# Q transposed contiguously and read by TensorE in the order of time, with chain steps ranked ahead of relus

## The chip, the cores and the metric

The kernel runs on one core of a Trainium2 chip. The core has five engines with a queue each: TensorE (PE in the profile, its weight loads PEld), VectorE (DVE), ScalarE (ACT), GpSimd (POOL) and SyncE (SP). Each engine takes its instructions in the order in which the program wrote them and waits where an operand isn't there yet; DMAs are issued from the queues of SP, ACT and POOL. The metric is the device time of one execution in microseconds, as the median of several runs.

## The reference

A gated recurrence (gateloop) over 768 steps for 4 batches and 8 heads of 48, with a complex decay clipped to magnitude 0.999, and behind it a dense block with relu squared over all 3072 tokens:

```python
mag = np.sqrt(a_re * a_re + a_im * a_im)
scale = np.minimum(mag, 0.999) / (mag + 1e-06)
a_re_n, a_im_n = (a_re * scale, a_im * scale)
for t in range(S):                       # S = 768
    new_re = ar * S_re - ai * S_im       # ar, ai: a_re_n, a_im_n at t
    new_im = ar * S_im + ai * S_re
    S_re, S_im = (new_re + k_t v_t^T, new_im)
    y[:, :, t] = q_t @ S_re
x = y.transpose(0, 2, 1, 3).reshape(3072, 384)
h = x @ w_in                             # 384 x 2048
g = np.maximum(h, 0.0) ** 2
out = g @ w_out                          # 2048 x 384
```

## The kernel before

All work is in `fast_path`; at its end a flag is computed from sums that were collected on the way, and a general version would run only if that flag were set.

The 3072 tokens are cut into six units of L = 512 tokens (n = 0 to 5), and a unit into W = 4 blocks of C = 128. For each unit there are three kinds of work.

`chain(n)` (rank CHAIN = 2) loads the decays, normalises them (`roots`, `normalise`), forms running products inside groups of four steps (`inner`), turns the totals with TensorE (`totals`, through the helper `turned`, L993, with copies by ScalarE at L1008), scans them on VectorE (`scan`), and turns them back (`back`, L993 and L1102). Its last part, `apply`, multiplies the running products into q and k (L1151 to L1189, with ScalarE's L1159, L1164 and L1169 between), and `gather` sends k to KC by DMA.

`pairs(n)` (rank PAIR = 1) works on two heads at a time, four pairs per unit. In units 0 and 1 (n < EARLY = 2) `turn_pe` transposes Q and K with TensorE (L1285) and ScalarE copies them to QT (L1288). From unit 2 on `turn` does it with VectorE's 32x32 stream transpose (L1262, two per pair: j = 0 is Q, j = 1 is K), and DMAs from SP and ACT put the blocks into QT (L1267). A row of four consecutive time steps lies side by side in the source, so each transpose writes its 32 results with a step of four elements, so that QT is in order of time: index (t c), c being the step within four. Then `score` multiplies K's columns with Q's (L1305), VectorE applies the causal mask (L1308), `keep` forms the block states (TensorE L1334, copies and sums by ScalarE L1344 and VectorE L1348), and `mix` adds scores times v (L1359) and state times Q (L1363) in PSUM. ScalarE copies the result to yt (L1371) and DMAs carry it to xT (L1378). Score and mix read Q as TensorE's moving operand and K as its weights.

`dense(n, grp)` (rank DENSE = 3) is the dense block of the unit in two groups of 256 tokens: x @ w_in (L1400), relu and square on ScalarE (L1431, L1432, rank (0, n), the first rank of all), and the second product, plain in unit 0 (L1446), by blocks in the others (L1497, with sums on VectorE at L1512 and L1521). It uses three PSUM banks d0 to d2. In unit 0 the weights, which come as 64-bit words, are also converted in pieces: ScalarE L809 and L813, VectorE L815 and L822.

What sets the order is a planner, the class `Plan`. Each piece of work is a `step` with an engine, an estimated duration, the keys it reads and writes, and a rank. The planner plays the steps through with these durations, fixed delays between engines (HOP, MARGIN, SLACK), a rate for DMAs, and takes on each engine the step of lowest rank among those that are ready; on VectorE and ScalarE it may hold an engine of low-ranked work a little (HOLD) for a step ranked ahead of URGENT = (2, 0.2). The program is then written out in that order, so every engine's queue is fixed before the run. The choice is made here:

```python
n = min((n for n in wait[e] if at[n] <= t), key=lambda n: (steps[n][4], n))
```

`steps[n][4]` is the rank. So a duration in a `step` call changes no instruction, only where instructions stand in the queues.

Of the kernel before, what the change touches and what calls it, by code (L numbers as in the profile page):

```python
# [598 lines left out]
def fast_path(ctx, tc, q, k, v, a_re, a_im, moe_w_in, moe_w_out, out, flag):  # L599
# [127 lines left out]
        return n / 1200.0 + 0.10  # L727

    SUM = 0.22
    SCORE = 0.7  # L730
    checked = []

    def step(*args, **kw):
        return plan.add(*args, **kw)

    def check(*args, **kw):
        checked.append(step(*args, **kw))
# [60 lines left out]
    def convert(i):  # L798
        held = [("a", 1)] if SOON <= i < NPIECE else []
        _, t, keys, dst, n, wk = piece(i)  # L800
        t3 = t.rearrange("p m (f two) -> p m f two", two=2)
        lo, hi = t3[:, :, :, 0], t3[:, :, :, 1]
        bits = dst.bitcast(U32)
        rank = (W2, 0.6) if i >= NPIECE else (W1, 0.3)
        def part(dtype, i):
            return t.bitcast(dtype).rearrange("p m (f four) -> p m f four", four=4)[:, :, :, i]

        step("ACT", ac(PW) + 0.06, keys, [("lo", i), ("lo", i, 0)],
             lambda: act.activation(out=lo, in_=lo, func=AF.Copy, scale=2.0 ** -29), rank)  # L809
        mixed = SOON <= i < 2 * NPIECE - 2  # L810
        if mixed:

            step("ACT", 1.92, keys + [("lo", i)], [("lo", i, 1)], lambda: act.activation(  # L813
                out=part(F16, 1), in_=part(I16, 3), func=AF.Copy, scale=2.0 ** -60), rank)
        step("DVE", ts2(PW), keys + held, wk, lambda: dve.tensor_scalar(  # L815
            out=bits, in0=hi, scalar1=0x07FFFFFF, scalar2=3,
            op0=ALU.bitwise_and, op1=ALU.logical_shift_left), rank)
        if not mixed:
            step("DVE", tt(PW), keys, wk, lambda: dve.scalar_tensor_tensor(
                out=bits, in0=hi, scalar=0xC0000000, in1=bits,  # L820
                op0=ALU.bitwise_and, op1=ALU.bitwise_or), rank)
        step("DVE", tt(PW), keys + [("lo", i, int(mixed))], wk, lambda: dve.tensor_tensor(  # L822
            out=bits, in0=bits, in1=lo, op=ALU.add), rank)
# [72 lines left out]
    def chain(n):  # L896
# [90 lines left out]
        def turned(src, put, by, keys, rk):  # L987
            b = trs[slot["tr"] % 2]
            slot["tr"] += 1

            def go():
                for m in range(NM):
                    pe.transpose(put(bank[b][:, 0:DM], m), src(m), by)  # L993
            step("PE", 0.12 * NM, keys, [(b,)], go, rk)
            return bank[b][:, 0:DM], (b,)

        def natural(t, m):
# [118 lines left out]
        def level():  # L1116
            dve.reciprocal(out=lv[:, n, 0:1], in_=tot[:, n:n + 1])
            dve.tensor_scalar(out=lv[:, n, 1:2], in0=lv[:, n, 0:1], scalar1=-UP * UP,
                              scalar2=None, op0=ALU.mult)
        check("DVE", 0.16, [("tot",)], [("lv", n)], level, ahead)  # L1120

        def squares(j):
            for r in range(2):
# [116 lines left out]
    def pairs(n, which):  # L1240
# [9 lines left out]
        def turn(i):  # L1250
            z = i // 2
            s = take("QT", 3 if 0 < n < ROOM else 2)
            t = QT[s].rearrange("p (i x) -> p i x", i=W)
            got["T", i] = s
            T6 = aq[z].rearrange("p (y j x) -> p y j x", y=2, j=NJ)
            for j in range(2):
                nat = ff[z][:, j * Z:(j + 1) * Z].rearrange(
                    "p (c h j r) -> p c h j r", c=W, h=HH, j=NJ)[:, :, ts(i % 2, 2)]
                dst = T6[:, i % 2].rearrange("p j (k h t c) -> p k c h j t", k=2, h=2, c=W)
                step("DVE", tt(768), [("f", z, 2 * j), ("f", z, 2 * j + 1)],  # L1260
                     [("a", z) if i % 2 == 0 else ("qk", z)],
                     lambda nat=nat, dst=dst, j=j: dve.transpose(out=dst[:, j], in_=nat), rank)  # L1262
            for b in range(W):
                for j in range(NJ):
                    queue = act if j == 2 else sp
                    dma(queue, [("a", z) if i % 2 == 0 else ("qk", z)], [("QT", s, 0), ("QT", s, 1)],
                        lambda b=b, j=j, z=z, t=t, T6=T6, queue=queue: queue.dma_start(  # L1267
                            out=t[32 * j:32 * j + 32, b],
                            in_=T6[32 * b:32 * b + 32, i % 2, j]), rank, 65536,
                        group=(n, i))  # L1270

        def turn_pe(i):
# [5 lines left out]
            for h in range(2):  # L1278
                for j in (1, 0):
# [3 lines left out]
                    def go(h=h, j=j, ps=ps):  # L1283
# [5 lines left out]
                        out=dst, in_=bank[b][0:R].rearrange("p (i t) -> p i t", i=W)), rank,  # L1289
                        group=(n, i))  # L1290

        def score(i, h):
            s = got["T", i]
            T = QT[s].rearrange("p (i k h t) -> p i k h t", i=W, k=2, h=2)[0:R]
            b = "sc%d" % take("sc", 2)
            sa = bank[b].rearrange("p (j t) -> p j t", j=W)
            a = take("A", 3 if 0 < n < ROOM else 2)
            got["A", i, h] = a

            def go():  # L1300
                for j0 in range(0, W, 2):
                    for half in range(2):
                        for j in (j0, j0 + 1):
                            p0, t0 = CH * (half ^ (j % 2)), CH * half
                            pe.matmul(sa[p0:p0 + CH, j, t0:C], lhsT=T[:, j, 1, h, t0:t0 + CH],  # L1305
                                      rhs=T[:, j, 0, h, t0:C], start=True, stop=True)
            step("PE", SCORE, [("QT", s, h)], [(b,)], go, rank, slack=True)
            step("DVE", tt(L) + 0.05, [(b,)], [("A", a)], lambda: dve.tensor_tensor(  # L1308
                out=As[a].rearrange("p (j o t) -> p j o t", o=2, t=C),
                in0=bank[b].rearrange("p (j o t) -> p j o t", o=2, t=C), in1=mask4,  # L1310
                op=ALU.mult), rank)

        def keep(i):
# [10 lines left out]
            for js in ([j for j in need if j < 3], [j for j in need if j == 3]):  # L1324
                if not js:
                    continue
                b = trs[take("tr", 2)]
                ps = bank[b][0:R, 0:8 * D].rearrange("p (j h d) -> p j h d", j=W, h=2)
                last = js == [3]

                def go(js=js, ps=ps):
                    for j in js:
                        for h in range(2):
                            pe.matmul(ps[:, j, h], lhsT=kc[:, j, (2 * i + h) % HH],  # L1334
                                      rhs=v5[:, j, 2 * i + h], start=True, stop=True)
                step("PE", 0.34 * len(js), [("KC%d" % last, z, i % 2), ("v", vs(n))], [(b,)], go,
                     rank, slack=True)

                for j in js:
                    o = new if j == 3 else at[j + 1]  # L1340
                    reads = [(b,)] + ([("S", n % 2, i)] if j == 0 else [("st", s, j)])
                    writes = [("S", (n + 1) % 2, i)] if j == 3 else [("st", s, j + 1)]
                    if at[j] is None:
                        step("ACT", ac(2 * D), reads, writes, lambda o=o, j=j, ps=ps: act.copy(  # L1344
                            out=o, in_=ps[:, j]), rank)
                    else:
                        step("DVE", tt(2 * D) + 0.04, reads, writes,
                             lambda o=o, j=j, ps=ps: dve.tensor_tensor(  # L1348
                                 out=o, in0=ps[:, j], in1=at[j], op=ALU.add), rank)

        def mix(i):
            T = QT[got["T", i]].rearrange("p (i k h t) -> p i k h t", i=W, k=2, h=2)[0:R]
            at, s = got["S", i]
            aa = [As[got["A", i, h]].rearrange("p (j t) -> p j t", j=W) for h in range(2)]

            def go():
                for j in range(W):
                    for h in range(2):
                        pe.matmul(ypair[64 * h:64 * h + D, ts(j, C)], lhsT=v5[:, j, 2 * i + h],  # L1359
                                  rhs=aa[h][:, j], start=True, stop=at[j] is None)  # L1360
                    for h in range(2):
                        if at[j] is not None:
                            pe.matmul(ypair[64 * h:64 * h + D, ts(j, C)], lhsT=at[j][:, h],  # L1363
                                      rhs=T[:, j, 0, h], start=False, stop=True)
            step("PE", 2.0, [("A", got["A", i, h]) for h in range(2)]
                 + [("v", vs(n)), ("QT", got["T", i], 0), ("QT", got["T", i], 1),
                    ("S", n % 2, i)]
                 + [("st", s, j) for j in (1, 2, 3)],
# [23 lines left out]
    def dense(n, grp):  # L1392
# [26 lines left out]
        for f2, b, ps, o, s in blocks:  # L1419
# [10 lines left out]
            def relu(o=o, ps=bank[b]):  # L1430
                act.activation(out=o, in_=ps, func=AF.Relu)  # L1431
                act.activation(out=o, in_=o, func=AF.Square)  # L1432
            step("ACT", 2 * ac(2 * G), [(b, "x"), (b,), (b, "y")],
                 [(b,)] + [("g", s, r) for r in range(4)], relu, (0, n))
        if n >= FAST:
            (seven if joint else eight)(n, grp)
# [56 lines left out]
    def half(n, b, r, h, w, wkeys, first=True, last=True):  # L1493

        def go():
            for j in range(4 * h, 4 * h + 4):
                pe.matmul(bank[b][:, 0:DH], lhsT=g4[:, r, j], rhs=w(j),  # L1497
                          start=first and j == 0, stop=last and j == NT - 1)
        step("PE", 1.32, gk(r, h) + wkeys, [(b,)], go, (DENSE, n))

    def w_lo(c):
        return lambda j: w2[:, j, ts(c, DH)]
# [186 lines left out]
```

## Time and profile before

| | |
|---|---|
| median of 3 runs | 706.53 us (705.7 to 707.09) |
| the profiled execution | 706.77 us, span 705.0 us |
| TensorE busy | 630.2 us (89%) |
| VectorE busy | 557.3 us (79%) |
| ScalarE busy | 339.5 us (48%) |
| mean granted TensorE clock | 0.991 |
| VectorE's stream transposes (L1262) | 32, 47.5 us |
| scores on TensorE (L1305, both shapes and targets) | 768 records |

Times in the profile count from the start of the span. Busy time of an engine leaves out waits. A row of a group names line, engine, operation, output and input with their shapes, then count, total busy time, mean in ns, and the idle time of the engine just before with what ended it. A row of the timeline begins with start and length in us and ends, in brackets, with the idle time before it and what released it. "x32" is a number of records; an fp32 matmul leaves two. A timeline's length of several matmuls goes from the first start to the last end, which is modelled, so matmuls overlap in it.

The first matmuls of any size start some 56 us into the span; units 0 and 1 reach their pairs near 56 and 170 us, units 2 to 5 near 270, 370, 470 and 575 us. After the last pairs, from about 616 us, only the dense block of unit 5 and the collected tests remain.

### The profile page before, as it was taken

How to read it: one execution, taken by the hardware profiler on the slowest of the kernel's cores; microseconds unless marked ns; L12 is line 12 of the kernel's file. 1: busy time of each engine (PE TensorE's matmuls, PEld its weight loads, DVE VectorE, ACT ScalarE, POOL GpSimd, SP SyncE). 2: the span in 40 equal slices, each digit the busy share in tenths (PEclk: the TensorE clock that was granted, in tenths of full speed). 3: DMA queues.
4: the chain of work that ended last, by engine and by line, in shares of the span. 5: the costliest groups of instructions: out<-in, count | busy, mean ns of one | idle time of the engine just before them, and what ended most of it. 6: DMA issues, size and time to landing. Idle time of an engine off the chain costs nothing.

```text
span 705.0 us, 11855 instructions
## 1 busy us (share of the span) xinstructions
PE 630.2 (89%) x4442; PEld 559.2 (79%) x4442; DVE 557.3 (79%) x1125; ACT 339.5 (48%) x586; POOL 96.3 (14%) x166
## 2 busy tenths in 40 slices
PE   0108898999999999989999999999999999999996
PEld 0007775686778999978998898988899988999996
DVE  7999992989787897885999698988887998336721
ACT  6678736865675153336453438435247352032230
POOL 6301140201100010120021030011030011032200
PEclk9999999999999999999999999999999999999999
DMA  9924386111630006562027580045561035287600
GB/s 285 332 99 101 68 224 191 24 45 45 169 98 5 12 16 156 145 168 68 13 66 185 138 178 8 1 101 146 135 164 18 23 92 141 51 279 253 240 3 27
DMA packets 52068, 79.53 MB, mean 113 GB/s; under 512 B 7745, under 2 KB 35073, under 8 KB 52001
## 3 DMA queue, kind: packets, MB, share of 16 engines
q0 software_dynamic: 11712, 40.90, 19.2%
q1 hardware_dynamic: 36160, 32.79, 18.8%
q10 hardware_dynamic: 4128, 4.98, 2.8%
q8 instruction: 37, 0.61, 0.4%
q14 instruction: 31, 0.25, 0.1%
HBM read 48.76 MB, written 4.72 MB: 76 GB/s over the span
## 4 chain that ended last, share of the span: by engine, by line
PE 61%; DVE 26%; DMA 6%; ACT 3%; issue 2%; SPq 1%; ACTq 0%; DVEq 0%
PE d L1400 21%; PE d L1497 20%; PE d L1446 5%; DVE aq L1262 4%; PE sc L1305 4%; DVE f L1189 3%; DMA aq<-in_q_dram 3%; DVE f L1151 3%; PE yp L1359 3%; PE tr L1334 2%; PE yp L1363 2%; DVE g L1512 2%; DVE aq L1155 2%; DVE KC L1038 1%; DMA QT<-aq 1%
## 5 line engine op out<-in xcount | busy, mean ns | idle before, releaser
L1400 PE MATMUL d<-xT,w 128*128 128x256 f32 x1056 | 237.7, 382 | 2.9 <-DMA xT<-yt 2.9
L1400 PEld LDWEIGHTS d<-xT,w 128*128 128x128 f32 x1056 | 199.6, 191 | 30.6 <-DMA xT<-yt 3.3
L1497 PE MATMUL d<-w,g 128*128 128x192 f32 x832 | 144.2, 329 | 0.0
L1497 PEld LDWEIGHTS d<-w,g 128*128 128x128 f32 x832 | 136.0, 191 | 2.1 <-issue 1.3
L1431 ACT ACTIVATE g<-d 128x512 f32<-128x512 f32 x88 | 52.4, 596 | 129.0 <-PE d L1400 111.2
L1432 ACT ACTIVATE g<-g 128x512 f32<-128x512 f32 x96 | 60.6, 631 | 3.0
L1512 DVE TENSOR_TENSOR g<-g 128x512 f32<-128x512 f32 x56 | 37.7, 687 | 30.6 <-ACT g L1432 18.6
L1497 PE MATMUL d<-T,g 128*128 128x192 f32 x336 | 59.6, 330 | 0.0
L1497 PEld LDWEIGHTS d<-T,g 128*128 128x128 f32 x336 | 56.0, 193 | 0.3
L1226 POOL DMA_DIRECT2D KC<-f x52 | 27.6, 545 | 174.9 <-DVE f L1189 125.3
L1458 POOL DMA_DIRECT2D out_dram<-ot x22 | 12.3, 559 | 278.1 <-DVE ot L1521 247.4
L1446 PE MATMUL d<-w,g 128*128 128x384 f32 x128 | 45.5, 505 | 3.1 <-DVE w L822 3.1
L1262 DVE STREAM_TRANSPOSE aq<-f 128x768 f32<-128x768 f32 x32 | 47.5, 1573 | 0.3
L1151 DVE TENSOR_TENSOR f<-aq,xn 128x384 f32<-128x384 f32 (+1 forms) x64 | 45.5, 749 | 1.4 <-ACT xn L1102 1.4
L1371 ACT COPY yt<-yp 112x512 f32<-112x512 f32 x24 | 13.9, 581 | 63.1 <-PE yp L1363 55.7
L1308 DVE TENSOR_TENSOR A<-sc,mask 128x512 f32<-128x512 f32 x45 | 29.8, 685 | 12.5 <-PE sc L1305 12.2
L1446 PEld LDWEIGHTS d<-w,g 128*128 128x128 f32 x128 | 24.4, 197 | 18.7 <-DVE w L822 3.7
L1305 PEld LDWEIGHTS sc<-QT 96*64 96x64 f32 x736 | 34.1, 137 | 5.6 <-issue 3.3
L1305 PE MATMUL sc<-QT 96*64 96x128 f32 (+1 forms) x736 | 37.4, 250 | 0.6 <-DMA QT<-aq 0.3
L964 DVE TENSOR_TENSOR f<-aq 128x384 f32<-128x384 f32 x72 | 36.9, 552 | 0.8
L1521 DVE TENSOR_TENSOR ot<-ot,d 128x192 f32<-128x192 f32 x61 | 20.7, 348 | 20.0 <-PE d L1497 19.7
L1359 PE MATMUL yp<-A,v 128*48 128x128 f32 x320 | 32.4, 277 | 3.5 <-DVE A L1308 3.3
(179 smaller groups left out, 919.5 us busy)
## 6 DMA issues: line engine op xcount, KB each, us to landing
QT<-aq SPq DMA_DIRECT2D x128, 64.0 KB, 2.0
f<-in_moe_w_in_dram POOLq DMA_DIRECT2D x8, 768.0 KB, 6.8
f<-in_moe_w_out_dram POOLq DMA_DIRECT2D x8, 768.0 KB, 6.8
out_dram<-ot POOLq DMA_DIRECT2D x22, 192.0 KB, 2.4
QT<-aq ACTq DMA_DIRECT2D x64, 64.0 KB, 2.1
KC<-f POOLq DMA_DIRECT2D x36, 96.0 KB, 3.4
xT<-yt SPq DMA_DIRECT2D x36, 96.0 KB, 2.6
aq<-in_a_re_dram SPq DMA_DIRECT2D x8, 384.0 KB, 4.1
```

Of the source, the lines that this page charges most:

```text
L964: lambda c=c, j=j: dve.tensor_tensor(out=f[j], in0=a[:, :, :, c - 1], in1=a[:, j, :, c].unsqueeze(1).to_broadcast([C, 2, HH, D]), op=ALU.m ...
L1151: lambda j=j, r=r: dve.tensor_tensor(out=f4[:, j, r], in0=a[:, r], in1=over(j), op=ALU.mult), late[z])
L1262: lambda nat=nat, dst=dst, j=j: dve.transpose(out=dst[:, j], in_=nat), rank)
L1305: pe.matmul(sa[p0:p0 + CH, j, t0:C], lhsT=T[:, j, 1, h, t0:t0 + CH], rhs=T[:, j, 0, h, t0:C], start=True, stop=True)
L1308: step("DVE", tt(L) + 0.05, [(b,)], [("A", a)], lambda: dve.tensor_tensor(out=As[a].rearrange("p (j o t) -> p j o t", o=2, t=C), in0=bank[ ...
L1359: pe.matmul(ypair[64 * h:64 * h + D, ts(j, C)], lhsT=v5[:, j, 2 * i + h], rhs=aa[h][:, j], start=True, stop=at[j] is None)
L1400: pe.matmul(ps, lhsT=w1[:, f // FP, m, ts(f % FP, C)], rhs=xT[:, n % 2, m, ts(grp, G)], start=(m == 0), stop=(m == NM - 1))
L1431: act.activation(out=o, in_=ps, func=AF.Relu)
L1432: act.activation(out=o, in_=o, func=AF.Square)
L1446: pe.matmul(ps, lhsT=gt[:, f % 2, ts(i, C)], rhs=w2[:, f], start=(f == 0), stop=(f == NF - 1))
L1497: pe.matmul(bank[b][:, 0:DH], lhsT=g4[:, r, j], rhs=w(j), start=first and j == 0, stop=last and j == NT - 1)
L1512: step("DVE", tt(4 * C), gk(x0, h) + gk(x1, h), gk(o, h), lambda: dve.tensor_tensor(out=g4[:, o, sl], in0=g4[:, x0, sl], in1=g4[:, x1, sl] ...
```

## The change

There are three things in the diff.

First, from unit 2 on the transpose of Q writes its 32 results next to each other: within QT, Q's index is now (c t) instead of (t c), while K's stays (t c). A new function `columns` gives `score` and `mix` views of Q and K; the view of Q walks c innermost, so TensorE still reads Q in order of time, now with a step of 32 elements (128 bytes) from one column to the next and four such steps per group. The results in PSUM are in the same order as before. Units 0 and 1 have Q in the old order and read it as before.

Second, `step` gives a new rank, (-1, ...), to every step outside VectorE whose function belongs to `apply`, `totals`, `back`, `turned` or `keep`, if its rank was (1, 1) or behind. These are the chain's late steps on ScalarE and TensorE in all units, and the state products with their copies from unit 1 on. They then come ahead of the relus' (0, n).

Third, several estimated durations are set anew; they enter the planner alone.

```diff
-    SCORE = 0.7
+    SCORE = 0.72
-    def step(*args, **kw):
-        return plan.add(*args, **kw)
+    FIRST = ("apply", "totals", "back", "turned", "keep")
+
+    def step(eng, dur, reads, writes, fn, rank, *args, **kw):
+        if eng != "DVE" and any(x in fn.__qualname__ for x in FIRST) and rank >= (PAIR, 1):
+            rank = (-1, rank[1])
+        return plan.add(eng, dur, reads, writes, fn, rank, *args, **kw)
...
-            step("ACT", 1.92, keys + [("lo", i)], [("lo", i, 1)], lambda: act.activation(
+            step("ACT", 1.65, keys + [("lo", i)], [("lo", i, 1)], lambda: act.activation(
...
-            step("PE", 0.12 * NM, keys, [(b,)], go, rk)
+            step("PE", 0.11 * NM, keys, [(b,)], go, rk)
...
-        check("DVE", 0.16, [("tot",)], [("lv", n)], level, ahead)
+        check("DVE", 0.26, [("tot",)], [("lv", n)], level, ahead)
...
-                dst = T6[:, i % 2].rearrange("p j (k h t c) -> p k c h j t", k=2, h=2, c=W)
-                step("DVE", tt(768), [("f", z, 2 * j), ("f", z, 2 * j + 1)],
+                dst = T6[:, i % 2].rearrange("p j (k h t c) -> p k c h j t" if j else
+                                             "p j (k h c t) -> p k c h j t", k=2, h=2, c=W)
+                step("DVE", 1.39 if j else tt(768), [("f", z, 2 * j), ("f", z, 2 * j + 1)],
...
+        def columns(s):
+            t6 = QT[s].rearrange("p (i k h %s) -> p i k h t c" % ("t c" if n < EARLY else "c t"),
+                                 i=W, k=2, h=2, c=W)[0:R]
+            return t6[:, :, 0], QT[s].rearrange("p (i k h t) -> p i k h t", i=W, k=2, h=2)[0:R, :, 1]
...
-                            p0, t0 = CH * (half ^ (j % 2)), CH * half
-                            pe.matmul(sa[p0:p0 + CH, j, t0:C], lhsT=T[:, j, 1, h, t0:t0 + CH],
-                                      rhs=T[:, j, 0, h, t0:C], start=True, stop=True)
+                            p0, t0 = CH * (half ^ (j % 2)), CH // W * half
+                            pe.matmul(sa[p0:p0 + CH, j, t0:], lhsT=kt[:, j, h, ts(half, CH)],
+                                      rhs=qt[:, j, h, t0:], start=True, stop=True)
-            step("DVE", tt(L) + 0.05, [(b,)], [("A", a)], lambda: dve.tensor_tensor(
+            step("DVE", tt(L), [(b,)], [("A", a)], lambda: dve.tensor_tensor(
...
-                            pe.matmul(ypair[64 * h:64 * h + D, ts(j, C)], lhsT=at[j][:, h],
-                                      rhs=T[:, j, 0, h], start=False, stop=True)
-            step("PE", 2.0, [("A", got["A", i, h]) for h in range(2)]
+                            pe.matmul(y4[64 * h:64 * h + D, j], lhsT=at[j][:, h],
+                                      rhs=qt[:, j, h], start=False, stop=True)
+            step("PE", 1.68, [("A", got["A", i, h]) for h in range(2)]
...
-            step("ACT", 2 * ac(2 * G), [(b, "x"), (b,), (b, "y")],
+            step("ACT", 2 * ac(2 * G) + 0.1, [(b, "x"), (b,), (b, "y")],
...
-        step("PE", 1.32, gk(r, h) + wkeys, [(b,)], go, (DENSE, n))
+        step("PE", 1.30, gk(r, h) + wkeys, [(b,)], go, (DENSE, n))
```

One more estimate, that of VectorE's sums of states (L1348), loses its 0.04.

More of the change, by code (lines that the diff above doesn't have):

```diff
@@ L1290, in turn_pe @@
                         group=(n, i))
+        def columns(s):
+            t6 = QT[s].rearrange("p (i k h %s) -> p i k h t c" % ("t c" if n < EARLY else "c t"),
+                                 i=W, k=2, h=2, c=W)[0:R]
+            return t6[:, :, 0], QT[s].rearrange("p (i k h t) -> p i k h t", i=W, k=2, h=2)[0:R, :, 1]
         def score(i, h):
             s = got["T", i]
-            T = QT[s].rearrange("p (i k h t) -> p i k h t", i=W, k=2, h=2)[0:R]
+            qt, kt = columns(s)
             b = "sc%d" % take("sc", 2)
-            sa = bank[b].rearrange("p (j t) -> p j t", j=W)
+            sa = bank[b].rearrange("p (j t c) -> p j t c", j=W, c=W)
             a = take("A", 3 if 0 < n < ROOM else 2)
@@ L1346, in keep @@
                     else:
-                        step("DVE", tt(2 * D) + 0.04, reads, writes,
+                        step("DVE", tt(2 * D), reads, writes,
                              lambda o=o, j=j, ps=ps: dve.tensor_tensor(
@@ L1351, in mix @@
         def mix(i):
-            T = QT[got["T", i]].rearrange("p (i k h t) -> p i k h t", i=W, k=2, h=2)[0:R]
+            qt, _ = columns(got["T", i])
+            y4 = ypair.rearrange("p (j t c) -> p j t c", j=W, c=W)
             at, s = got["S", i]
```

## The prediction

> **What bounds the kernel now.** I read the page's busy shares first, then the span by stage, then every gap in TensorE's timeline, and last the rows of the instructions that the change touches.
>
> ```profile
> PE 630.2 (89%) x4442; PEld 559.2 (79%) x4442; DVE 557.3 (79%) x1125; ACT 339.5 (48%) x586; POOL 96.3 (14%) x166
> ```
>
> That is the headline; the table by stage tells more. Columns: stretch, its length, busy time of PE, PEld, DVE, ACT and POOL (instructions in brackets), granted clock, DMA share, GB/s.
>
> ```profile
> 60.00:140.00 80.00, 73.61 (x525) 56.48 (x525) 64.83 (x114) 53.45 (x87) 14.54 (x21) 0.98 0.50 128
> 140.00:260.00 120.00, 119.18 (x794) 100.24 (x793) 101.67 (x247) 67.62 (x129) 9.08 (x17) 1.00 0.21 58
> 260.00:320.00 60.00, 57.11 (x508) 52.41 (x507) 48.83 (x72) 22.81 (x37) 9.84 (x16) 0.98 0.60 149
> 365.00:412.00 47.00, 44.96 (x439) 40.61 (x438) 39.80 (x60) 19.25 (x35) 8.36 (x15) 1.00 0.65 157
> 412.00:465.00 53.00, 53.00 (x292) 49.68 (x291) 48.43 (x118) 26.50 (x51) 4.03 (x8) 1.00 0.26 55
> 465.00:520.00 55.00, 52.35 (x467) 47.77 (x466) 44.84 (x66) 22.72 (x40) 4.74 (x9) 0.97 0.49 123
> 570.00:616.00 46.00, 44.42 (x441) 40.12 (x440) 33.17 (x49) 9.18 (x17) 3.42 (x7) 1.00 0.45 109
> 616.00:705.00 89.00, 83.17 (x449) 77.60 (x448) 40.34 (x77) 20.58 (x35) 14.27 (x21) 0.99 0.46 159
> ```
>
> From 140 us on TensorE is the bound: it is full in the stretches where one unit's dense block runs beside the next unit's chain (412 to 465), and it loses 2.89, 2.04, 2.65 and 1.58 us in the four stretches where the pairs of units 2 to 5 are worked (260 to 320, 365 to 412, 465 to 520, 570 to 616). A faster VectorE is worth only what it takes out of those gaps. These are the gaps; the bracket gives TensorE's idle time and what ended it:
>
> ```profile
> 122.43 4.54 PE L1446 MATMUL d<-w,g 128*128 128x384 f32 x8 [3.13 <-DVE w L822]
> 315.82 10.99 PE L1400 MATMUL d<-xT,w 128*128 128x256 f32 x42 [2.89 <-DMA xT<-yt]
> 382.67 0.53 PE L1359 MATMUL yp<-A,v 128*48 128x128 f32 x5 [1.57 <-DVE A L1308]
> 396.77 1.19 PE L1305 MATMUL sc<-QT 96*64 96x128 f32 x22 [0.34 <-DMA QT<-aq]
> 475.27 1.22 PE L1334 MATMUL tr<-v,KC 128*96 128x48 f32 x12 [0.91 <-ACT St L1344]
> 496.49 1.22 PE L1334 MATMUL tr<-v,KC 128*96 128x48 f32 x12 [1.74 <-ACT St L1344]
> 587.16 0.42 PE L1359 MATMUL yp<-A,v 128*48 128x128 f32 x2 [0.63 <-DVE A L1308]
> 593.89 0.81 PE L1359 MATMUL yp<-A,v 128*48 128x128 f32 x3 [0.67 <-DVE A L1308]
> ```
>
> All but the first lie in units 2 to 5 and sum to 8.75 us. The granted clock adds a little: 0.98 of 60 us and 0.97 of 55 us in the two stretches with the longest gaps, that is 1.2 + 1.7 = 2.9 us. So about 11.7 us of the span is all that a relieved VectorE could return in units 2 to 5.
>
> **The change part by part.**
>
> ```profile
> L1262 DVE STREAM_TRANSPOSE aq<-f 128x768 f32<-128x768 f32 x32 | 47.5, 1573 | 0.3
> L925 DVE TENSOR_TENSOR f<-f 128x768 f32<-128x768 f32 x12 | 11.5, 955 | 10.2 <-ACT f L922 10.0
> L1305 PE MATMUL sc<-QT 96*64 96x128 f32 x368 | 34.2, 279 | 0.6 <-DMA QT<-aq 0.3 <-ACT QT L1288 0.2
> L1363 PE MATMUL yp<-QT,St 96*48 96x128 f32 x248 | 25.7, 272 | 0.0
> L1285 PE MATMUL tr<-ident,f 128*96 128x128 f32 x64 | 8.5, 276 | 0.8 <-ACT QT L1288 0.8
> 169.65 0.87 PE tr L1285 x8
> 275.63 1.49 PE sc L1305 x32
> 621.01 20.72 PE d L1400 x96
> 283.15 2.80 PE d L1497 x16
> L1082 DVE TENSOR_TENSOR KC<-e,yt 128x384 f32<-128x384 f32 x24 | 12.3, 551 | 0.2
> L1087 DVE TENSOR_TENSOR xn<-KC 128x384 f32<-128x384 f32 x12 | 9.7, 810 | 0.4
> ```
>
> The rows are groups with their mean in ns, and four-word rows from the chain of waits: start, length, what, records. TensorE's fp32 matmul counts as two records.
>
> (1) VectorE's transposes. There are 32 of 1573 ns, four pairs in each of units 2 to 5, one of Q and one of K per pair. Each writes with a step of 16 bytes; the 16 of Q will write runs of 32 elements. No contiguous transpose is in the trace. The bounds are 1573 ns (the step is not what costs) and 955 ns, what a tensor_tensor of the same 768 elements takes. I take 955, the nearest row with contiguous output: 16 x 0.62 = 9.9 us of VectorE, 2.5 us in each unit. The DMAs from aq to QT stay as many and as large.
>
> (2) TensorE's reads of Q, in units 2 to 5 alone: the moving operand of all scores (4 units x 4 pairs x 32 records = 512) and of the state matmuls (64 + 48 + 48 + 64 = 224 records, as units 3 and 4 start or cross a batch). It is now read in steps of 128 bytes. No row shows such a read. Upper bound: VectorE's own price for steps, 1573 / 955 = 1.65, on all of TensorE's time in them. 32 score records take 1.49 us, so 512 take 23.8 us; at the 109 ns of 169.65 (128 columns), and two heads side by side, 224 take 12.2 us; 36 x 0.65 = 23 us slower. Lower bound: nothing; reading in steps can't be quicker than in a row. The nearest row on this engine is L1285, which writes PSUM in steps of 16 bytes: 0.87 / 8 = 109 ns for 128 columns, 0.85 ns a column, while the dense L1400, all contiguous, takes 20.72 / 96 = 216 ns for 256 columns, 0.84 ns. A step costs TensorE nothing there, so I take 0 and keep 23 us as the far end.
>
> The Trainium skill (Advanced Engine Details and Errata, Memory Cachelines) says that any non-contiguous PSUM pattern slows matmuls significantly, and that SBUF has 16-byte lines of which each should be hit twice to run at full speed. On PSUM the trace disagrees at this fp32 pace (109 ns against 216 for double the columns); on an SBUF read in steps no run here shows it yet. By the first finding the term is 0, by the rule it is a rival, below.
>
> (3) What the quicker transposes and the new order do to the gaps. Ahead of the gaps VectorE has:
>
> ```profile
> 380.54 1.55 DVE L1262 STREAM_TRANSPOSE aq<-f 128x768 f32<-128x768 f32 x1
> 465.72 5.79 DVE L1262 STREAM_TRANSPOSE aq<-f 128x768 f32<-128x768 f32 x4
> 488.30 3.01 DVE L1262 STREAM_TRANSPOSE aq<-f 128x768 f32<-128x768 f32 x2
> 491.75 2.93 DVE L1262 STREAM_TRANSPOSE aq<-f 128x768 f32<-128x768 f32 x2
> 584.97 1.62 DVE L1262 STREAM_TRANSPOSE aq<-f 128x768 f32<-128x768 f32 x1
> ```
>
> Half of these are Q's. If nothing else moved, the gap at 382.67 would lose about 0.6, at 475.27 all 0.9 (two Q transposes ahead), at 496.49 1.2, at 396.77 all 0.3, at 587.16 and 593.89 0.5 each. At 315.82 TensorE has run out of other work while the last pair's rows travel to xT. The new order puts 4 matmuls of L1497 (8 records; the chain of waits has 16 in 2.80 us, so 1.4 us) behind the last mix of unit 2 where none stood, and the last pair comes some 1.2 us sooner: 2.4 off 2.89. Sum 6.4 of 8.75. The planner however orders the DVE, ACT and PE queues anew with every cost it is given, and states (L1334) are moved ahead of dense work, so a part of these gaps will come back elsewhere: I count two thirds, 4.3 us, and of the 2.9 us of clock 1 us.
>
> (4) ScalarE's and TensorE's chain steps ranked first. ScalarE is 48% busy and no gap of TensorE waits for a relu, so a relu later by one chain step (1.5 us at most, L922 below) is covered by the three d banks: price 0. If that cover went, TensorE would wait on d banks, which it does nowhere now. TensorE's moved steps are the same instructions at other places: 0. The POOL queue keeps its order but for a few places, and SP's changes only with the pairs.
>
> (5) The order around 120 us. ScalarE's queue there:
>
> ```profile
> 115.34 1.48 ACT L922 ACTIVATE f<-aq 128x1536 f32<-128x1536 f32 x1 [5.07 <-DMA aq<-in_q_dram]
> 117.96 0.91 ACT L809 ACTIVATE QT<-QT 128x768 uint32<-128x768 uint32 x1
> 119.50 1.88 ACT L813 ACTIVATE QT<-QT 128x768 f16<-128x768 int16 x1
> 121.42 0.96 DVE L822 CUSTOM_DVE_ANT_0 w<-QT,w 128x1536 uint16<-128x1536 uint16 x1 [3.04 <-ACT QT L813]
> L927 ACT ACTIVATE f<-f 128x768 f32<-128x768 f32 x12 | 10.1, 840 | 10.2 <-DVE f L925 6.1 <-DVE St L1348 4.1
> ```
>
> L922 waits 5.07 us for its load, and the conversion of the fourth w2 piece (L809, L813, L822) is queued behind it; TensorE then waits 3.13 us for that piece. In the new order the piece's L809 and two relus stand ahead of L922 and its L813 straight behind it, so L813 starts near 117.0, not 119.5: 2.5 us sooner. The next piece is then what TensorE waits for: L927, L809, L929 (of L927's kind) and L813 take about 0.8 + 0.9 + 0.8 + 1.9 = 4.4 us more, and the new queue takes its matmuls before the six dense ones that filled this hole. I count 2 us of the 2.5.
>
> (6) The other costs (SCORE, the mix, transposes, levels, relu) change no instruction, only places. Queue order up to 56 us is nearly the same, and TensorE does little there: 0.
>
> Sum: 0 (reads) - 4.3 (gaps) - 1.0 (clock) - 2.0 (unit 1) = -7.3; I leave 1 us for waits that the new order makes in units 0 and 1, where TensorE lost 6.4 us of 80 and VectorE is as full. That is -6.3 on the profiled execution's 706.77 us (span 705.0): 700.5, and as the median stood 0.24 lower at 706.53, 700.3.
>
> **The rivals.**
>
> A, slower: TensorE's reads in steps of 128 bytes are not free. By the DVE ratio above the price is 23 us on the engine that bounds; all gaps of units 2 to 5 then vanish under it, and 706.8 + 23 - 7 gives 723. It decides from 6.3 / 36 = 18% per matmul on. For it speaks VectorE's 1573 ns, a real price of steps on this memory; against it L1285 and that an fp32 column occupies TensorE for 0.84 ns, time enough to fetch one element. The Trainium skill's SBUF rule (Advanced Engine Details and Errata, Memory Cachelines) would give this case, as every element lies in another line. I give it 27%.
>
> B, the gain does not come: the gaps are made by where a static queue meets a late arrival, not by VectorE's total, so the new queues have as many. For it: the gaps have five different releasers; two are ScalarE's copies and two are DMAs. Against: four of eight stand right behind a transpose. Then 704 to 709, near 706.5. 15%.
>
> C, within the forecast: the transposes stay at 1573 because the 32x32 turn costs, not the step. For it: no contiguous one is seen. Against: L1087, which writes 384 elements in steps of 64 bytes, takes 810 ns, and L1082, which writes as many in a row, 551. Only the order's 3 us would be left: 703.5.
>
> **How the numbers follow.** The forecast, with C inside it, has 58% and its own range 695 to 705: all 11.7 us back at one end, 2 us at the other. A has 27% (708 to 725), B 15% (704 to 709). The range 694 to 725 leaves out some 10%. A difference of 0.2% (1.4 us) is about what a measurement can tell from none: faster is 57 of the forecast's 58 and 4 of B's 15; within 0.2% the other 1 and 7 of B; slower the last 4 of B and A's 27.
>
> **What would show it.** Right: the transposes fall into two groups, near 0.95 and 1.57 us; 32 score records of units 2 to 5 still take 1.5 us and a mix 1.7; the wait before L1446 near 120 falls below 1.5 us; TensorE's idle time between 140 and 620 falls from some 10 us to about 5. Wrong: score records of 70 ns pitch and more against 47 (A), or as many gaps at other lines (B).

## The result: 2.8% slower

| | before | after |
|---|---|---|
| median | 706.79 us (4 runs, 705.7 to 707.09) | 726.32 us (4 runs, 723.98 to 729.13) |
| the profiled execution | 706.77 us, span 705.0 us | 729.13 us, span 727.4 us |
| ratio, after to before | | 1.0279, 95% interval 1.0245 to 1.0312 |

The forecast was 700.3 us with a range of 694 to 725; the measured time lies 1.3 us above its upper end. What happened is rival A, with a larger price than it was given.

The profile after, first the page's busy shares, then the stages in which the pairs of units 2 to 5 are worked (columns as in the table of before):

```profile
PE 663.5 (91%) x4442; PEld 576.5 (79%) x4442; DVE 552.4 (76%) x1125; ACT 340.7 (47%) x586; POOL 96.3 (13%) x166
```

```profile
260.00:330.00 70.00, 70.00 (x531) 60.24 (x530) 50.16 (x77) 25.22 (x42) 9.84 (x16) 1.00 0.50 127
370.00:425.00 55.00, 55.00 (x450) 45.96 (x449) 38.35 (x61) 22.38 (x40) 6.98 (x11) 1.00 0.51 126
480.00:540.00 60.00, 60.00 (x475) 51.85 (x474) 45.91 (x70) 21.44 (x38) 7.77 (x12) 1.00 0.53 138
590.00:640.00 50.00, 50.00 (x432) 42.42 (x431) 27.06 (x45) 7.58 (x13) 2.12 (x4) 1.00 0.37 90
```

TensorE has as many records as before (4442) and is 33 us longer busy. In these stages it has no gap at all, where it had 9.16 us of them, and the clock is full. So the lost time is not waiting: it is work that takes longer. The groups of the changed kernel show which (with shapes kept apart; total busy, then mean in ns), and the chain of waits and the timeline further down show the pitch, the time from one record to the next:

```profile
L1315 PE MATMUL sc<-QT 96*64 96x128 f32 x368 | 53.5, 377 | 0.0
L1374 PE MATMUL yp<-QT,St 96*48 96x128 f32 x248 | 35.2, 358 | 0.0
L1267 DVE STREAM_TRANSPOSE aq<-f 128x768 f32<-128x768 f32 x32 | 39.2, 1271 | 0.2
L1318 DVE TENSOR_TENSOR A<-sc,mask 128x512 f32<-128x512 f32 x45 | 31.0, 690 | 37.2 <-PE sc L1315 37.1
```

The mask's row before, for comparison:

```profile
L1308 DVE TENSOR_TENSOR A<-sc,mask 128x512 f32<-128x512 f32 x45 | 29.8, 685 | 12.5 <-PE sc L1305 12.2
```

The chain of waits and the timeline of the changed kernel:

```profile
277.80 2.89 PE sc L1315 x32
```

```profile
303.59 2.87 PE L1508 MATMUL d<-w,g 128*128 128x192 f32 x16
306.39 0.43 PE L1370 MATMUL yp<-A,v 128*48 128x128 f32 x4
...
309.22 1.57 PE L1508 MATMUL d<-w,g 128*128 128x192 f32 x8
```

L1315 is the score (L1305 before) and L1374 the state product (L1363 before). 32 score records take 2.89 us instead of 1.49; a mix with 16 state records lasts from 306.39 to 309.22, 2.83 us. The transposes did what the change says: their mean of 1271 ns is that of 16 at about 1570 and 16 at about 970. And VectorE now stands idle for 37 us in front of the mask, waiting for scores, where it was 12.5 us before.

### The profile page after: what moved, and what is told of

Its sections match the earlier page's. It is cut to its first block, busy times and chain, and to the rows that moved or that the text cites. A ratio compares the mean times of both kernels' runs of the same rounds, so it can differ in the third digit from the quotient of the medians.

```text
span 727.4 us, 11863 instructions
## 1 busy us (share of the span) xinstructions
PE 663.5 (91%) x4442; PEld 576.5 (79%) x4442; DVE 552.4 (76%) x1125; ACT 340.7 (47%) x586; POOL 96.3 (13%) x166
## 4 chain that ended last, share of the span: by engine, by line
PE 82%; DVE 10%; DMA 4%; ACT 1%; SPq 1%; issue 1%; DVEq 0%; ACTq 0%
PE d L1411 29%; PE d L1508 26%; PE sc L1315 8%; PE d L1457 5%; PE yp L1374 4%; PE tr L1344 3%; PE yp L1370 3%; DMA aq<-in_q_dram 3%; DVE f L968 1%; PE d L1290 1%; DMA aq<-in_a_im_dram 1%; DVE aq L950 1%; PE tr L997 1%; PE sc L1411 1%; PE tr L1411 1%; PE tr L1290 1%
## 5 line engine op out<-in xcount | busy, mean ns | idle before, releaser
L1508 PE MATMUL d<-w,g 128*128 128x192 f32 x832 | 144.0, 328 | 0.0
L1315 PE MATMUL sc<-QT 96*64 96x128 f32 (+1 forms) x736 | 60.6, 326 | 0.0
L1315 PEld LDWEIGHTS sc<-QT 96*64 96x64 f32 x736 | 47.9, 152 | 12.1 <-issue 2.1
L1230 POOL DMA_DIRECT2D KC<-f x52 | 27.7, 546 | 178.2 <-DVE f L1193 132.3
L1267 DVE STREAM_TRANSPOSE aq<-f 128x768 f32<-128x768 f32 x32 | 39.2, 1271 | 0.2
L1374 PE MATMUL yp<-QT,St 96*48 96x128 f32 x248 | 35.2, 358 | 0.0
```

Source lines behind the costliest of these rows:

```text
L1315: pe.matmul(sa[p0:p0 + CH, j, t0:], lhsT=kt[:, j, h, ts(half, CH)], rhs=qt[:, j, h, t0:], start=True, stop=True)
L1374: pe.matmul(y4[64 * h:64 * h + D, j], lhsT=at[j][:, h], rhs=qt[:, j, h], start=False, stop=True)
L1508: pe.matmul(bank[b][:, 0:DH], lhsT=g4[:, r, j], rhs=w(j), start=first and j == 0, stop=last and j == NT - 1)
```

## The experiments

### The parts one by one

The layout alone (ranks and estimates of before, Q contiguous, TensorE reading in steps):

```diff
-                dst = T6[:, i % 2].rearrange("p j (k h t c) -> p k c h j t", k=2, h=2, c=W)
+                dst = T6[:, i % 2].rearrange("p j (k h t c) -> p k c h j t" if j else
+                                             "p j (k h c t) -> p k c h j t", k=2, h=2, c=W)
...
+                                      rhs=qt[:, j, h, t0:], start=True, stop=True)
...
+                                      rhs=qt[:, j, h], start=False, stop=True)
```

> The layout alone: Q is transposed contiguously and TensorE reads it in steps of 128 bytes as in the changed kernel, but ranks and estimates, and so nearly all queue orders, are those of the kernel before. Theory 1 (the read in steps costs TensorE time): 32 score records of units 2 to 5 take 2.9 us as in the changed kernel, a mix 2.7, 36 us more on TensorE less some 10 us of gaps that close: 728 to 735. Theory 2 (the new queue order is what costs; the long records are waits that the profile shows as work): records at 1.5 us and 698 to 706.

Measured: 733.95 us, ratio 1.0361 (1.03 to 1.0423). Its chain of waits has the long scores, and its timeline still the old order's longest gap:

```profile
604.79 2.90 PE sc L1311 x32
```

```profile
328.80 10.83 PE L1407 MATMUL d<-xT,w 128*128 128x256 f32 x42 [3.22 <-issue]
```

The kernel before, run beside it, took 706.23 us. So the layout by itself costs 27.7 us, 8 more than the whole change (19.5), and the order should gain.

The order alone (ranks and estimates of after, Q written and read as before):

```diff
-                dst = T6[:, i % 2].rearrange("p j (k h t c) -> p k c h j t" if j else
-                                             "p j (k h c t) -> p k c h j t", k=2, h=2, c=W)
+                dst = T6[:, i % 2].rearrange("p j (k h t c) -> p k c h j t", k=2, h=2, c=W)
...
-            ... ("t c" if n < EARLY else "c t") ...
+            ... "t c" ...
```

> The order alone: ranks, estimates and all queue orders of the changed kernel, but Q is written and read as before, in order of time with a 16-byte step on VectorE. Theory 1: TensorE's records as before (1.5 us per 32 scores), VectorE's transposes all at 1.57 us, time 702 to 708. Theory 2: 720 and more.

Measured: 695.13 us, ratio 0.9816 (0.9763 to 0.9869), 7 us faster than the lower end of theory 1. The stages, in the stretches used for the kernel before:

```profile
260.00:320.00 60.00, 60.00 (x527) 55.18 (x526) 50.97 (x74) 24.50 (x41) 9.85 (x16) 1.00 0.57 144
365.00:412.00 47.00, 47.00 (x451) 42.95 (x450) 40.45 (x66) 20.72 (x37) 7.27 (x12) 1.00 0.65 149
465.00:520.00 55.00, 54.75 (x487) 50.13 (x486) 49.07 (x79) 24.71 (x43) 7.79 (x12) 1.00 0.61 162
570.00:616.00 46.00, 45.81 (x442) 42.21 (x442) 25.79 (x43) 6.58 (x12) 6.45 (x11) 1.00 0.47 124
```

9.16 us of gaps have become 0.44, with the transposes no quicker than before (mean 1601 ns against 1573). What comes from unit 2 on can be measured apart from the start, from the point at which TensorE first turns unit 2's decays; before, then here:

```profile
226.67 0.49 PE L993 MATMUL tr<-perm,xn 128*128 128x128 f32 x3
```

```profile
227.41 0.49 PE L997 MATMUL tr<-perm,xn 128*128 128x128 f32 x3
```

From there to the end of the span, 478.3 us (705.0 - 226.67) have become 466.3 (693.7 - 227.41): 12.0 us, and the gaps with the clock came to 11.7.

The changed kernel with TensorE reading the columns as they lie ("in line" from here on; seen as (t c), data that lie as (c t) are read in a row):

```diff
-            t6 = QT[s].rearrange("p (i k h %s) -> p i k h t c" % ("t c" if n < EARLY else "c t"),
+            t6 = QT[s].rearrange("p (i k h %s) -> p i k h t c" % "t c",
```

> The changed kernel in every respect, contiguous transposes and queue order included, but TensorE reads Q's 128 columns in the order in which they lie, so the columns of each block are not those of the right time steps and the result is not the reference's. It leaves nothing out but the order of the columns. Theory 1: score records back to 1.5 us per 32; the time is what was predicted for free reads, 698 to 704. Theory 2: 720 and more, as the order is that of the changed kernel.

Measured: 690.78 us, ratio 0.9778 (0.9727 to 0.9829). The chain of waits has

```profile
586.89 1.49 PE sc L1315 x32
```

This is 7 us below what was expected for free reads, since the order gains more than the prediction gave it. TensorE, VectorE and ScalarE work through the same lines in the same order in the traces of the changed kernel and of this run; the transposes are the same, and only the step of TensorE's reads is taken away: 726.32 becomes 690.78. That is the price of the reads, 35.5 us, and it rules out theory 2. Counted from unit 2's turn of the decays, in the changed kernel and here, the price is nearly the same: 499.9 us (727.4 - 227.54) become 464.7 (688.7 - 223.99), 35.2 us.

```profile
227.54 0.49 PE L997 MATMUL tr<-perm,xn 128*128 128x128 f32 x3
```

```profile
223.99 0.49 PE L997 MATMUL tr<-perm,xn 128*128 128x128 f32 x3
```

### What in the read costs

Two variants of the kernel before, in which TensorE reads Q's columns in steps of two elements (b=64), then of four (b=32 in the same line):

```diff
+            t6 = QT[s].rearrange("p (i k h b a) -> p i k h a b", i=W, k=2, h=2, b=64)[0:R]
...
+                                      rhs=qt[:, j, h, t0:], start=True, stop=True)
```

> The kernel before, but every score and every state product, in all units, reads Q's 128 columns in steps of two elements (8 bytes: 64 even columns, then 64 odd ones), so the result is not the reference's; nothing is left out. If the cost belongs to leaving a 16-byte line at each column, two columns share a line here and 32 score records stay at 1.5 us, time 703 to 709. If any step other than one element costs, they take 2.9 us and the time is above 735, as units 0 and 1 pay too.

> As the run with 8-byte steps, but TensorE reads Q's columns in steps of four elements (16 bytes), so that each column lies in another 16-byte line; the order of columns is not the reference's and nothing is left out. If leaving the line is what costs, 32 score records take 2.9 us in every unit and the time is near 750 (1.5 times the 36 us of four units, less the gaps of 12 us); if only longer steps cost, 1.5 us and 703 to 710.

Measured: 709.86 us with 8 bytes, 749.42 us with 16 (one execution each). The chains of waits, 8 bytes first:

```profile
280.60 1.53 PE sc L1309 x32
```

```profile
288.94 2.88 PE sc L1309 x32
```

Eight bytes cost 0.04 us in 1.49; sixteen cost as much as 128 do. The Trainium skill (Advanced Engine Details and Errata, Memory Cachelines) says of SBUF that a 16-byte line should be hit at least twice; this trace agrees, with 1.53 us at two columns to a line and 2.88 at one. No run shows whether the cost belongs to leaving 16 bytes that lie together or to the length of the step: a step between 8 and 16 bytes was not tried.

### What made the order gain

The new ranks alone, then the new estimates alone, both with Q as before:

```diff
+    FIRST = ("apply", "totals", "back", "turned", "keep")
+    def step(eng, dur, reads, writes, fn, rank, *args, **kw):
+        if eng != "DVE" and any(x in fn.__qualname__ for x in FIRST) and rank >= (PAIR, 1):
+            rank = (-1, rank[1])
```

> The kernel before with the new ranks alone: Q written and read as before, all estimates as before. It splits the 11 us that the order alone took off (695.1 against 706.2). If the ranks did it, 694 to 698; if the estimates did, 703 to 708; if both share it, between.

> The kernel before with the new estimates alone, ranks, layout and reads as before. If the estimates made the 11 us, 694 to 698; if the ranks did, 703 to 708.

Measured: ranks 699.64 us, ratio 0.993 (0.9877 to 0.9982); estimates 713.91 us, ratio 1.0091 (1.0063 to 1.0119). The ranks gain a part, 7 us by the medians (1 to 9 by the interval), which lies between the two guesses; the estimates by themselves lose 7, which fits neither guess. Together they gain 11 to 15. Two rows of the run with the estimates alone show a new hole between 520 and 570 us, where TensorE was full before (50.00 of 50.00), and a wait at the end of unit 2's pairs as before:

```profile
520.00:570.00 50.00, 46.37 (x280) 42.28 (x276) 44.80 (x111) 25.20 (x47) 5.10 (x7) 0.97 0.29 70
```

```profile
322.39 10.99 PE L1406 MATMUL d<-xT,w 128*128 128x256 f32 x42 [3.60 <-issue]
```

So the two don't add up; a static order is made by both at once. Why just this pair of changes closes all gaps stays open. (The planner goes through its engines in the order of a Python set, so ties can fall differently from one build of the same source to the next. They do: the reads in line were built twice, and 24 of 4442 matmul records and 29 of 1125 VectorE instructions stand at other places in the second trace. The medians of the two, 690.78 and 689.84 us, are 1 us apart.)

### VectorE's relief by itself, and a version without the price

VectorE's contiguous transposes in the kernel before, with reads in line:

```diff
+                dst = T6[:, i % 2].rearrange("p j (k h t c) -> p k c h j t" if j else
+                                             "p j (k h c t) -> p k c h j t", k=2, h=2, c=W)
...
+            t6 = QT[s].rearrange("p (i k h %s) -> p i k h t c" % "t c",
```

> The kernel before with its own ranks, estimates and queue order, and only VectorE's Q transposes made contiguous; TensorE reads the columns in the order in which they lie, at no step, so the columns of each block are not those of the right time steps and the result is not the reference's; nothing is left out. This is the relief of VectorE by itself, on which the prediction's largest term rests (4.3 us of gaps and 1.0 of clock out of the old order). If the relief closes gaps as predicted: 700 to 703. If the gaps are set by where the queues meet and not by VectorE's total: 705 to 707.

Measured: 702.56 us, ratio 0.9922 (0.9891 to 0.9954). The stages:

```profile
260.00:320.00 60.00, 57.22 (x515) 52.79 (x514) 47.01 (x70) 23.82 (x38) 9.85 (x16) 1.00 0.59 146
365.00:412.00 47.00, 46.19 (x444) 41.62 (x443) 38.43 (x62) 20.18 (x35) 8.49 (x14) 1.00 0.68 159
465.00:520.00 55.00, 53.95 (x483) 49.02 (x482) 45.97 (x71) 22.28 (x39) 6.27 (x10) 1.00 0.55 143
570.00:616.00 46.00, 45.61 (x455) 42.09 (x454) 27.35 (x47) 7.57 (x13) 4.93 (x9) 1.00 0.44 106
```

9.16 us of gaps have become 5.03. What stays is mostly the 2.78 us at the end of unit 2's pairs, which the order closes and the transposes don't:

```profile
316.71 9.30 PE L1407 MATMUL d<-xT,w 128*128 128x256 f32 x42 [2.78 <-issue]
```

A version that keeps Q contiguous on both sides: all units write Q as (c t), TensorE reads and writes columns in that order, the mask is built for it, and the output DMA puts the rows back.

```diff
-                                      rhs=qt[:, j, h, t0:], start=True, stop=True)
+                                      rhs=qt[:, j, h, :, t0:], start=True, stop=True)
...
+            part = part.rearrange("p (c t) -> p c t", c=W)
+            pool.affine_select(out=part, in_=part, pattern=[[1, W], [W, C // W]], ...
...
-            out=out[r:r + C, :], in_=ots[o]), (DENSE, n), C * DM * 4)
+            out=out[r:r + C, :].rearrange("(t c) e -> c t e", c=W), in_=ots[o]), ...
```

> The changed kernel with Q contiguous on both sides: transposes write Q as (c t) in all units, TensorE reads and writes its columns in that order (runs of 16 or more elements), the mask is built for it, and the DMAs that write the output put the rows back in order. Theory 1: score records at 1.5 us per 32, transposes of Q at 0.95 us, time 688 to 695, no gap above 0.5 us from 140 us on; a mask or DMA that costs would show as waits of L1318 or at the end of the span.

Measured: 694.79 us, ratio 0.9822 (0.9785 to 0.9859). The order alone, the reads in line and this version lie within a few us of one another. All three once more, on one chip:

> The order alone once more, beside the two below on one chip, as its distance to them is a few us: 693 to 696.

> The changed kernel with TensorE reading the columns as they lie, once more (the result is not the reference's). If VectorE's relief still helps under the new order, 4 us below the order alone (689 to 692); if TensorE has no gap left to give, within 1.5 us of it.

> Q contiguous on both sides with the rows put back by the output DMA, once more. As fast as the run above if the output DMAs and the mask cost nothing (within 1.5 us); some 3 us above it if they do.

Measured: the order alone 692.57 us, ratio 0.978 (0.9756 to 0.9804); reads in line 689.84 us, 0.9761 (0.9736 to 0.9785); contiguous on both sides 692.85 us, 0.9782 (0.9759 to 0.9804). The reads in line are 2.7 us below the order alone, which lies between the two distances expected, and 3.0 us below the version contiguous on both sides, but the intervals overlap. Counted from unit 2's turn of the decays the profiled executions of the order alone need 466.3 and 466.2 us, those of the reads in line 464.7 and 464.1: about 2 us are left for VectorE's relief under the new order. The profiled executions of the last two are 7.1 us apart. Of these, 5.4 are there when the last dense block starts, and 3.9 of them already at unit 2's turn; only the rest, at the end, can be put to the output DMA. Start of the last dense block and span, in line first:

```profile
663.67 18.21 PE d L1508 x112
...
span 687.6 us, 11867 instructions
```

```profile
669.05 18.21 PE d L1511 x112
...
span 694.7 us, 11863 instructions
```

From there it is 23.9 us to the end with the plain output DMA and 25.6 us with the one that puts rows back: 1.7 us that belong to the last rows. Both versions with right results, the order alone and Q contiguous on both sides, are 11 to 15 us faster than the kernel before in the two sets of runs, and no difference between them shows.

## Why the prediction was wrong, point by point

**The bound** was read rightly: TensorE from 140 us on, with 11.7 us of gaps and clock in units 2 to 5 as the most that a relieved VectorE could return. From unit 2's turn of the decays on the order alone returned 12.0 us, and the order with the relief and the reads in line 13.6 (478.3 to 464.7), so the bound was about right, if a little low.

**Step 1, the transposes**: right. 16 x 0.62 = 9.9 us were taken off VectorE by estimate; the means give 32 x (1573 - 1271) ns = 9.7 us, and the group's busy time, which counts overlaps once, went from 47.5 to 39.2 us, 8.3.

**Step 2, TensorE's reads in steps: this is the step that failed.** It said "a step costs TensorE nothing there, so I take 0". The row it leaned on, L1285, writes PSUM in steps; the change reads SBUF in steps, and a free write to the one memory said nothing of a read from the other. The measured price is 35.5 us in place of 0, and it can be put together: 512 score records at 1.40 us more per 32 are 22.4; a mix with 16 state records took 2.83 us where it takes 1.90 with the order alone (rows below), so 224 records cost 224 / 16 x 0.93 = 13.0 us. Sum 35.4.

```profile
297.72 2.87 PE L1507 MATMUL d<-w,g 128*128 128x192 f32 x16
302.42 1.57 PE L1507 MATMUL d<-w,g 128*128 128x192 f32 x8
```

(16 records of L1507 take 2.80 us, so the mix between these rows runs from 300.52 to 302.42.) The far end of the range was too short as well: VectorE's ratio of 1.65 gave 23 us, TensorE's own is 2.89 / 1.49 = 1.94.

**Step 3, the relief**: near in its sum, in part by luck. 4.3 us of gaps and 1.0 of clock were forecast; alone the relief closed 4.1 us of gaps and took 4.9 us off the median. But the 4.3 were two thirds of 6.4, of which 2.4 were to come from the end of unit 2's pairs, where the new order was to help, and the relief alone returned 0.1 there. From the other gaps it returned 4.0, all that was forecast before the third was taken off. It was wrong that the order would add "1 us for waits that the new order makes": alone the order took 11 to 15 us off, in two sets of runs. With both, 15 to 18 us; what one closes the other can't close again.

**Step 4, ranks at no price**: right that no relu or d bank became a wait, but the ranks alone took 7 us off the median, and the step looked for a cost alone.

**Step 5, the order near 120 us**: 2 us were forecast, and a wait below 1.5 us. TensorE still waits 2.49 us there, and ScalarE's L926 (L922 before), behind which the piece's conversion is queued, starts at 118.65 instead of 115.34, when its load lands:

```profile
118.65 1.48 ACT L926 ACTIVATE f<-aq 128x1536 f32<-128x1536 f32 x1 [3.23 <-DMA aq<-in_q_dram]
...
123.07 8.30 PE L1457 MATMUL d<-w,g 128*128 128x384 f32 x20 [2.49 <-DVE w L826]
```

Most of that delay is not the order's: this execution was already 3 us late from TensorE's start (last section). The reads in line have the same queues and an early start:

```profile
116.16 1.48 ACT L926 ACTIVATE f<-aq 128x1536 f32<-128x1536 f32 x1 [3.71 <-DMA aq<-in_q_dram]
...
120.57 6.82 PE L1457 MATMUL d<-w,g 128*128 128x384 f32 x20 [2.97 <-DVE w L826]
```

There TensorE gets the piece at 120.57 instead of 122.43, 1.9 us sooner and near the forecast. But the wait stays at 2.97 us, because TensorE also runs out of other matmuls sooner, at 117.60 instead of 119.30. What the step had wrong is that a piece that is ready sooner shortens the wait by as much.

**The rivals.** A had the right mechanism, the right sign to watch for (records at 70 ns pitch and more; they came at 90) and 723 us, near the 726.3. It came near by luck, because two misses offset each other: the price was 12 us short, and the gains against it were 9 us short. C is out: the contiguous transpose is quick. B's outcome is out too, as the gaps closed, but its mechanism is in part borne out: the order alone took the gaps from 9.16 to 0.44 us with the transposes no quicker, while the relief in the old order closed less than half of them. What stood against A was "time enough to fetch one element" in 0.84 ns a column; with the columns 16 bytes or more apart the scores took 1.9 times as long.

## What to carry to other kernels

Here a step that was taken off one engine's write was put on another engine's read, and its price must be looked for per memory and per direction: a step that cost nothing in a write to PSUM said nothing of a read from SBUF. Keep at least two fp32 columns of a moving operand in each 16 bytes, or carry the odd order through (here up to the output DMA, at 1.7 us, where it came out no faster than the old layout). And test an order and a layout apart: here the gain of one, 11 to 15 us, was hidden under the price of the other, 35.5.

## What the runs showed of the hardware

TensorE's start differs from execution to execution by some 3 us. The same 12 transposes behind the first scores, before and after (in both the granted clock of that stretch is given as 1.00):

```profile
63.24 1.48 PE L1285 MATMUL d<-ident,f 128*96 128x128 f32 x12
...
141.01 0.82 PE L993 MATMUL tr<-perm,xn 128*128 128x128 f32 x6
```

```profile
64.95 2.76 PE L1290 MATMUL d<-ident,f 128*96 128x128 f32 x12
...
144.12 0.82 PE L997 MATMUL tr<-perm,xn 128*128 128x128 f32 x6
```

In the second execution the records run at about half pace until 68 us, in the first only until 61, with the first matmul at 56.1 in both; at unit 1's turn of the decays it is 3.1 us behind. It does not hang on the source alone: of the two runs of Q contiguous on both sides, the first has these transposes at 2.76 us and the second at 1.48. The reads in line have the short start (140.6 at the same place) and the order alone the long one (144.0) in the executions profiled first, so part of the few us between them is this. The granted clock between 100 and 140 us adds its part: it is 1.00 in both profiled executions of the reads in line, and 0.96 and 0.91 in those of the order alone. The Trainium skill (TensorE: Matmul & The Clock Gate, Part 1: The HAM clock gate) puts the change of pace at about 4 us into sustained work, half a microsecond more or less; these traces show 5 and 12 us, with the gaps of the first pairs small in both. What sets the two starts apart was not tried.
